# Half blocks of x for the column loop, issued by ScalarE instead of SyncE

## The chip, the cores and the metric

The kernel runs on one core of a Trainium2 chip. A core has five engines that each work through their own list of instructions in order: TensorE (PE, with PEld for its weight loads), VectorE (DVE), ScalarE (ACT), GpSimd (POOL) and SyncE (SP), which only issues transfers and waits. Transfers run on the core's 16 DMA engines. Engines wait for one another, and for transfers, by semaphores. The metric is the time of one execution on the device in microseconds; less is better.

## The reference

For four sequences of 12,608 positions with 128 channels, a long convolution by FFT is multiplied by x, and a mixture-of-experts step then rewrites the 128 positions of each sequence that score highest:

```
h = (relu(pos_emb @ w1) @ w2) * exp(-0.01 * pos)[:, None]
y = irfft(rfft(x * v, 2S) * rfft(h, 2S), 2S)[:, :S]
a = x * y                                    # the "column loop" makes this product
scores = a @ w_gate                          # per sequence
top = argpartition(-scores, 128)[:128]
out = a;  out[top] += sigmoid(scores[top]) * (relu(a[top] @ w1e) @ w2e)
```

## The kernel before

The transform of length 93 * 250 is taken apart into small matrix products. The work of one sequence (b, four of them) falls into two parts.

**Groups.** 32 groups of four channels each, so 128 turns t in all; the loop over t is in the body of the kernel. In one turn each engine does a few operations of different groups:

- PE: the last transform of group i = t - 3 (`f_i`, L546), the middle transform of group t (`dft`, L341), the first transform of group t + 1 (`f_s1`, L481).
- ACT: copies L546's banks out of PSUM (L550, L551), copies half of L341's result (L344, which DVE's L490 needs), copies L481's result to SBUF (two L483, which the next turn's L341 on PE needs). During the turns of sequences 1 to 3 it also carries the search for the 128 highest scores of the sequence before, a round a turn (L871, L874, L887).
- DVE: the product with the filter's spectrum (`f_y`, L497 to L501) and sums and differences (L490, L487).
- POOL: the product x * v (`stage_u`, L324), L508, L509 and two L589.
- SP: per turn two loads of x and v (`load_u`, L318), one or two stores or two loads of the filter's spectrum (L1305, or `load_h`, L330), in three of four turns a move inside SBUF (`put`, L562).

**Column loop.** After the 32 groups, `P1.run` goes over 16 blocks of columns: the closing transform (L636), the product with x (L647), scores (L691, L701), the store (L675). Its x comes by `load_a` (L611) into a ring of buffers. Six of the blocks have buffers that are free early; these are loaded ahead, in 12 half blocks (4 columns each, 112 partitions x 512 values, 224 KB), one each at the end of the turns listed in `LA`: turns 18 to 29 of sequence 0, every second turn from 6 to 28 of sequences 1 to 3. So there are 48 such half blocks. The other blocks are loaded inside `run`.

**What orders the transfers.** Each engine's list is in the order in which the code records it. All transfers that SP issues draw on eight completion semaphores, DMAHW0 to DMAHW7, handed out in turn over the whole program. A transfer takes the next semaphore and waits, before it is issued, until the transfer that used that semaphore last, the eighth one before it, has landed. It also waits for whatever frees its buffer.

Of the kernel before, what the change touches and what calls it, by code (L numbers as in the profile page):

```python
# [30 lines left out]
HB = 4  # L31
# [9 lines left out]
PR, P0, SH = 112, 8, 13  # L41
# [34 lines left out]
AHEAD = [i for i in range(NX + 3) if XB[i] not in XE]  # L76
# [162 lines left out]
def hyena_moe(ctx, tc, xg, x2, pos, bw, ww, wg, mw1, mw2, cs, c1, gx, cf, ci, wm, tk, out):  # L239
    nc = tc.nc  # L240
# [9 lines left out]
    def view(t, off, shape):  # L250
        n = int(np.prod(shape[1:]))
        r = t[:shape[0], off:off + n]
        if len(shape) > 2:
            ax = "abcdefg"[:len(shape) - 1]
            r = r.rearrange(f"p ({' '.join(ax)}) -> p {' '.join(ax)}", **dict(zip(ax[1:], shape[2:])))
        return r
# [57 lines left out]
    def load_u(t):  # L314
        b = t // NG
        if b < B:
            for k, n in enumerate("xv"):
                nc.sync.dma_start(buf(n, t, [NP, XC]), xg[b, :, GC[t], k])  # L318

    def stage_u(t):  # L320
        if t >= B * NG:
            return
        x, v = buf("x", t, [NP, XC]), buf("v", t, [NP, XC])
        nc.gpsimd.tensor_tensor(out=x, in0=x, in1=v, op=ALU.mult)  # L324
# [13 lines left out]
    def dft(t, te, pq):  # L338
        for w in (1, 0):
            for a in range(0, 128, 32):  # L340
                nc.tensor.matmul(pq[w][a:a + 32], lhsT=cf_sb[:, 2 * w + a // NQ, a % NQ:a % NQ + 32],  # L341
                                 rhs=te[:, a // NQ], start=True, stop=True)
        qs = buf("qs", t, [128, HC])
        nc.scalar.copy(out=qs, in_=pq[1])  # L344
        return qs
# [129 lines left out]
    def f_s1(t, dst=None, ps=bank1):  # L475
        u = buf("x", t, [NP, 4, N3])
        te = buf("te", t, [128, 2, 4, N1]) if dst is None else dst
        tps = [view(ps[h], 0, [128, 2, 2, N1]) for h in range(2)]
        for s in range(4):
            for k, c in enumerate(BLK):  # L480
                nc.tensor.matmul(tps[s // 2][c, s % 2], lhsT=u[:, s, c], rhs=c1_sb[:, k], start=True, stop=True)  # L481
        for h in range(2):
            nc.scalar.copy(out=te[:, :, 2 * h:2 * h + 2].rearrange("p e s i -> p s e i"), in_=tps[h])  # L483
        return te.rearrange("p e s i -> p e (s i)")

    def f_u(pq, qs):
        nc.vector.tensor_tensor(out=nat(pq[0]), in0=nat(pq[0]), in1=rev(qs), op=ALU.add)  # L487

    def f_v(pq, qs):
        nc.vector.tensor_tensor(out=nat(pq[1]), in0=rev(pq[0]), in1=nat(qs), op=ALU.subtract)  # L490

    def f_y(t, uv):
        ht = buf("ht", HI[t], [128, 2, HC]) if HS[t] != "hh" else hh[:, GC[t]].rearrange("p e s i -> p e (s i)")
        mt, yz = buf("mt", t, [128, 2, HC]), buf("yz", t, [128, 2, HC])
        for e in (1, 0):
            for o, k in ((mt[:, e], 0), (uv[e], 1)):
                nc.vector.tensor_tensor(out=o, in0=uv[e], in1=ht[:, k], op=ALU.mult)  # L497
        yield yz
        nc.vector.tensor_tensor(out=yz[:, 0], in0=uv[1], in1=mt[:, 0], op=ALU.add)  # L499
        yield yz  # L500
        nc.vector.tensor_tensor(out=yz[:, 1], in0=mt[:, 1], in1=uv[0], op=ALU.subtract)  # L501
        yield yz
# [61 lines left out]
    def turn(i):  # L564

        g, r = i % NG, i % 4
        if i > DIR:
            u = [(t, s) for t in ((i, DIR) if i == DIR + 1 else (i,)) for s in range(4)]
        elif r == 0:
            u = [(i - 1, s) for s in (1, 2, 3)] if g else []  # L570
        else:
            u = {1: [(i, 0), (i, 1), (i, 2)], 2: [(i - 1, 3), (i, 0), (i, 1)], 3: [(i - 1, 2), (i - 1, 3), (i, 0)]}[r]
            if g == NG - 1:
                u += [(i, s) for s in (1, 2, 3)]
        done = []
        for t, s in u:
            f_i(t, s)
            if s == 3:
                done.append(t)
                if t % NG >= NG - 3 and t < DIR:  # L580
                    o, i = parts(t, (0, JM))
                    nc.scalar.copy(out=o, in_=i)
        return done
# [10 lines left out]
    class P1:  # L594
# [7 lines left out]
            self.pw = self.nw = 0  # L602
            self.late = []

        def load_a(self, i, a=0, z=8):
            if i < len(ORD):
                k = ORD[i]
                j0, j1 = blocks[k]
                z = min(z, j1 - j0)
                self.xa[k] = view(arena, XB[i], [128, 8, D])  # L610
                nc.sync.dma_start(self.xa[k][P0:P0 + PR, a:z], x2[self.b, :, j0 + a:j0 + z])  # L611

        def comb(self):
            k = next(self.more, None)
# [622 lines left out]
    te, uv, ys, sd, ph = {}, {}, {}, {}, {}  # L1237
# [7 lines left out]
    def small_steps():  # L1245
        for _ in range(ND):
            bg.hook("d")

    for t in range(NT + LAG):
        g = t % NG  # L1250
        i = t - LAG
        bg.now = t
        done = turn(i) if i >= 0 else []
        if t < NT:
            pq = [bank2[2 - 2 * (t % 2) + e] for e in range(2)]
            spare[0] = [a[:, 512 - NS:] for a in bank1]
            uv[t] = [a[:, :HC] for a in pq]
            qs = dft(t, te.pop(t), uv[t])
            if t == 0:
                rest()  # L1260
            bg.hook("p", 2)
            spare[0] = [pq[0][:, HC:]]
            bg.hook("t", 1)
            spare[0] = [a[:, 512 - NS:] for a in bank1]
            bg.hook("n", 1)
            for k in ((1, 2), (3,), (4,), (5,), ())[t] if t < 5 else (t + 1,):
                if k < NT:
                    te[k] = f_s1(k, ps=banks[6:] if k == 2 else bank1)
            spare[0] = None
            if t != 4:  # L1270
                load_u(t + NU + (t < 4))
            if 0 <= t - 4 < len(fills):
                z = fills[t - 4]
                nc.scalar.activation(out=z, in_=one.to_broadcast([128, z.shape[1]]), func=AF.Copy, scale=0.0)
            o = t - 1 in uv
            if o:
                steps = f_y(t - 1, uv.pop(t - 1))
                y = next(steps)
                next(steps)
            end = t == NT - 1  # L1280
            if end:
                next(steps)
            else:
                small_steps()
            f_v(uv[t], qs)
            if o and not end:
                next(steps)
            if not end:
                bg.hook("e")
            f_u(uv[t], qs)  # L1290
            seam = i >= 0 and i % NG == NG - 1
            now = [k for k in done if seam or end or k % NG == NG - 3]
            done_ = [k for k in done if k not in now]
            for k in now:
                f_c(k)
            if o or t - 1 in ys:
                sd[t - 1] = f_sd(t - 1, y if o else ys.pop(t - 1))
            for k in done_:
                f_c(k, (ALU.subtract,))
            if not seam and t != 4:  # L1300
                stage_u(t + 3 + (t < 4))
            for k in done_:
                f_c(k, (ALU.add,))
            for k in range(4 * (t - 1) // 3, min(4 * t // 3, NG)) if t else ():
                nc.sync.dma_start(hd[:, k], hh[:, k].rearrange("p e s i -> p (e s i)"))  # L1305
            load_h(t + 2)
            for k in due + [k for k in done if k % NG >= NG - 3]:
                put(k, *((JM, NJ) if k % NG >= NG - 3 else ()))
            due = [k for k in done if k % NG < NG - 3]
            for _ in range(0 if end else NE):  # L1310
                bg.hook("e")
            if i >= 0 and i % NG == NG - 1:
                *_, ys[t] = f_y(t, uv.pop(t))
            if t == NT - 1:
                sd[t] = f_last(t, uv.pop(t))
        if t >= NT:
            for k in due:
                put(k)
            due = []
            for k in done:  # L1320
                f_c(k)
        if t == NT:
            bg.drain()
            ex = Experts(picked)
        b = i // NG
        if i >= 0 and i % NG in LA[b]:
            if i % NG == LA[b][0]:
                ph[b] = P1(b)
            k, e = divmod(LA[b].index(i % NG), 2)
            ph[b].load_a(AHEAD[k], e * HB, (e + 1) * HB)  # L1330
        if i % NG == NG - 1 and i >= 0:
            bg.drain("w")
            p1 = ph.pop(b)
            p1.run(ex)
            bg.drain()
            bg = Background(topk_one(b, p1, ex))
# [51 lines left out]
```

## Time and profile before

| | us |
|---|---|
| median of three timed runs | 778.36 (775.6 to 780.43) |
| the profiled execution, its own time | 783.39 |
| its span, first to last instruction | 781.6 |
| PE busy | 760.4 (97% of the span) |
| DVE busy | 684.9 (88%) |
| POOL busy | 619.5 (79%) |
| ACT busy | 572.1 (73%) |

The profiled execution took 5.03 us (0.6%) more than the median, and 1.79 us of it lie outside the span. Busy shares are means over the group turns, the column loops and the two ends of the program. TensorE's granted clock is 0.999 of full speed over the whole run. All transfers of the program stand on one hardware queue that SP feeds, and its packets take 79.8% of the 16 DMA engines' span.

### The profile page before, as it was taken

What the parts mean: (1) busy time and instruction counts of PE and PEld (TensorE: products, weight loads), DVE (VectorE), ACT (ScalarE), POOL (GpSimd) and SP (SyncE); (2) the same over time, 40 slices, a digit from 0 to 9 for tenths busy, and PEclk for the clock granted to TensorE, in tenths of its full rate; (3) what the DMA queues carried; (4) which work ended last, traced back from release to release, by engine and by line L of the source; (5) the groups of instructions that cost most, each with busy time, mean ns of one, the idle gap of its engine ahead of it and who ended that gap; (6) DMA issues with size and microseconds to landing.
All of it is one profiled execution on the core that took longest, in us unless ns stands there. A gap on an engine that the chain in (4) does not pass through costs nothing. (4 is left out here: it accounts for less than half of the span.)

```text
span 781.6 us, 37672 instructions
## 1 busy us (share of the span) xinstructions
PE 760.4 (97%) x15191; PEld 560.6 (72%) x15191; DVE 684.9 (88%) x1549; ACT 572.1 (73%) x2286; POOL 619.5 (79%) x704
## 2 busy tenths in 40 slices
PE   8999999999999999999999999999999999999996
PEld 8999767888853677877834777789536778877356
DVE  7468699989989899989899998989998998997992
ACT  0324567756569989886679898986699888975892
POOL 0200189999989799998888899989997998998873
PEclk9999999999999999999999999999999999999999
DMA  9200269999889979999789999999789899995780
GB/s 323 78 28 3 81 226 297 301 305 288 225 276 286 315 242 290 284 280 270 210 261 304 292 264 279 285 269 265 237 275 330 250 275 270 273 272 163 251 298 26
DMA packets 95649, 190.44 MB, mean 244 GB/s; under 512 B 11952, under 2 KB 70256, under 8 KB 95472
## 3 DMA queue, kind: packets, MB, share of 16 engines
q1 hardware_dynamic: 95216, 187.48, 79.8%
q8 instruction: 121, 1.98, 1.1%
q0 software_dynamic: 256, 0.52, 0.2%
q14 instruction: 56, 0.46, 0.2%
HBM read 135.34 MB, written 41.35 MB: 226 GB/s over the span
## 5 line engine op out<-in xcount | busy, mean ns | idle before, releaser
L546 PE MATMUL b<-ci_sb,arena 128*31 128x126 f32 x6096 | 206.6, 270 | 4.4 <-issue 3.8
L341 PE MATMUL c<-arena,cf_sb 128*32 128x372 f32 x2032 | 201.9, 477 | 3.5 <-issue 2.6
L481 PE MATMUL a<-c_sb,arena 128*32 128x186 f32 x4064 | 202.3, 322 | 2.4 <-issue 2.2
L324 POOL TENSOR_TENSOR arena<-arena 128x500 f32<-128x500 f32 x128 | 162.6, 1271 | 46.1 <-DMA arena<-in_xg_dram 23.9
L546 PEld LDWEIGHTS b<-ci_sb,arena 128*31 128x31 f32 x6096 | 184.0, 109 | 12.9 <-issue 6.9
L508 POOL TENSOR_TENSOR arena<-arena 128x372 f32<-128x372 f32 x127 | 116.5, 917 | 80.6 <-DVE arena L501 72.1
L483 ACT COPY arena<-a 128x372 f32<-128x372 f32 x252 | 119.7, 475 | 80.5 <-PE a L481 75.6
L481 PEld LDWEIGHTS a<-c_sb,arena 128*32 128x32 f32 x4064 | 149.0, 109 | 39.0 <-issue 17.7
L701 ACT ACTIVATE arena<-arena 128x128 f32<-128x128 f32 x490 | 143.8, 295 | 13.0 <-DVE arena L691 12.5
L550 ACT COPY big<-b 128x412 f32<-128x412 f32 x192 | 108.3, 565 | 12.4 <-PE b L546 10.5
L509 POOL TENSOR_TENSOR arena<-arena 128x372 f32<-128x372 f32 x127 | 116.1, 914 | 0.0
L341 PEld LDWEIGHTS c<-arena,cf_sb 128*32 128x32 f32 x2032 | 83.1, 109 | 45.9 <-issue 23.0
L589 POOL TENSOR_TENSOR big<-big,arena 128x184 f32<-128x184 f32 x194 | 112.8, 583 | 1.3
L497 DVE TENSOR_TENSOR c<-c,arena 128x372 f32<-128x372 f32 x188 | 102.4, 545 | 0.0
L497 DVE TENSOR_TENSOR arena<-c,arena 128x372 f32<-128x372 f32 x188 | 100.8, 536 | 0.0
L701 ACT ACTIVATION_READ_ACCUMULATOR arena<-arena 128x1 f32 x490 | 91.7, 187 | 0.0
L490 DVE TENSOR_TENSOR c<-c,arena 128x372 f32<-128x372 f32 x128 | 70.3, 550 | 20.5 <-ACT arena L344 14.2
L621 POOL TENSOR_TENSOR arena<-big 96x512 f32<-96x512 f32 x64 | 79.3, 1267 | 0.1
L636 PE MATMUL a<-big,gx_sb 96*64 96x512 f32 (+2 forms) x448 | 75.9, 474 | 1.4 <-DVE arena L647 0.8
L344 ACT COPY arena<-c 128x372 f32<-128x372 f32 x128 | 60.9, 476 | 14.8 <-PE c L341 14.2
L487 DVE TENSOR_TENSOR c<-c,arena 128x372 f32<-128x372 f32 x128 | 70.0, 547 | 0.2
L499 DVE TENSOR_TENSOR arena<-c,arena 128x372 f32<-128x372 f32 x127 | 68.1, 536 | 0.0
(222 smaller groups left out, 1079.8 us busy)
## 6 DMA issues: line engine op xcount, KB each, us to landing
arena<-in_xg_dram SPq DMA_DIRECT2D x256, 250.0 KB, 5.0
arena<-hd SPq DMA_DIRECT2D x178, 186.0 KB, 5.3
out_dram<-arena SPq DMA_DIRECT2D x60, 448.0 KB, 5.6
arena<-in_x_dram SPq DMA_DIRECT2D x36, 448.0 KB, 5.1
hd<-big SPq DMA_DIRECT2D x32, 372.0 KB, 5.1
arena<-in_x_dram SPq DMA_DIRECT2D x48, 224.0 KB, 5.4
big<-big SPq DMA_DIRECT2D x84, 126.0 KB, 5.0
big<-in_pos_dram SPq DMA_DIRECT2D x7, 496.0 KB, 7.0
```

The lines of the kernel that those rows point to most:

```text
L324: nc.gpsimd.tensor_tensor(out=x, in0=x, in1=v, op=ALU.mult)
L341: nc.tensor.matmul(pq[w][a:a + 32], lhsT=cf_sb[:, 2 * w + a // NQ, a % NQ:a % NQ + 32], rhs=te[:, a // NQ], start=True, stop=True)
L481: nc.tensor.matmul(tps[s // 2][c, s % 2], lhsT=u[:, s, c], rhs=c1_sb[:, k], start=True, stop=True)
L483: nc.scalar.copy(out=te[:, :, 2 * h:2 * h + 2].rearrange("p e s i -> p s e i"), in_=tps[h])
L497: nc.vector.tensor_tensor(out=o, in0=uv[e], in1=ht[:, k], op=ALU.mult)
L508: eng.tensor_tensor(out=nat(sd[:, 0]), in0=nat(yz[:, 0]), in1=rev(yz[:, 1]), op=ALU.add)
L509: eng.tensor_tensor(out=nat(sd[:, 1]), in0=rev(yz[:, 0]), in1=nat(yz[:, 1]), op=ALU.subtract)
L546: nc.tensor.matmul(o3[32 * k:32 * k + NT3, s % 2, e * NJ + js.start:e * NJ + js.stop], lhsT=d[:, e, s, c], rhs=ci_sb[:, e, js], start=True ...
L550: nc.scalar.copy(out=ay[:, GC[t], :NJ + JM, ss], in_=o3[:, :, :NJ + JM].rearrange("p s x -> p x s"))
L589: nc.gpsimd.tensor_tensor(out=d if op == ALU.subtract else a[:, :n], in0=a[:, :n], in1=stg(t)[:, :n], op=op)
L621: nc.gpsimd.tensor_tensor(out=cm[:KP, e].rearrange("p j (g s) -> p j g s", s=4), in0=av[0], in1=av[1], op=op)
L701: nc.scalar.activation(out=x, in_=x, func=AF.Copy, accum_out=self.sc[:, j:j + 1])
```

## The change

`load_a` gets a parameter for the issuing engine, with SyncE as the default, and the call in the group turns passes ScalarE. The calls inside `run` stay on SyncE.

```
-        def load_a(self, i, a=0, z=8):
+        def load_a(self, i, a=0, z=8, eng=nc.sync):
...
-                nc.sync.dma_start(self.xa[k][P0:P0 + PR, a:z], x2[self.b, :, j0 + a:j0 + z])
+                eng.dma_start(self.xa[k][P0:P0 + PR, a:z], x2[self.b, :, j0 + a:j0 + z])
...
             k, e = divmod(LA[b].index(i % NG), 2)
-            ph[b].load_a(AHEAD[k], e * HB, (e + 1) * HB)
+            ph[b].load_a(AHEAD[k], e * HB, (e + 1) * HB, nc.scalar)
```

PE, DVE and POOL keep their lists. ACT's list gains 48 transfers, SP's loses them.

ACT before, between two turns of sequence 1 (L871 and L874 belong to the search's round; `b` is a PSUM bank of L546, `c` of L341, `a` of L481; `ms`, `hi` and `st` hold the search's counts and bounds):

```order
L871 ACTIVATE ms_0_3935,st_3937<-hi_3934,st_3937 128x126 [waits Activation_49]
L874 ACTIVATE st_3937<-tk_sb,st_3937 128x4
L550 COPY big<-b_76 128x206x2 [waits PE_49]
L551 COPY arena<-b_76 128x46x2 [waits Pool_49]
L344 COPY arena<-c_75 128x372 [waits PE_49]
```

ACT of the change, at the same place:

```order
L871 ACTIVATE ms_0_3935,st_3937<-hi_3934,st_3937 128x126 [waits Activation_49]
L874 ACTIVATE st_3937<-tk_sb,st_3937 128x4
L611 DMA arena<-in_x_dram 112x512 [waits DMAHW3_49]
L550 COPY big<-b_76 128x206x2 [waits PE_49]
L551 COPY arena<-b_76 128x46x2 [waits Pool_49]
L344 COPY arena<-c_75 128x372 [waits PE_49]
L483 COPY arena<-a_70 128x2x2x93 [waits PE_49]
L483 COPY arena<-a_71 128x2x2x93 [waits PE_49,Activation_49]
```

The half block's load stands ahead of the next turn's three kinds of copies, with a wait for the last transfer on DMAHW3.

SP before, at the same place of the program:

```order
L330 DMA arena<-hd 128x372 [waits DMAHW1_49,DVE_49]
L330 DMA arena<-hd 128x372 [waits DMAHW2_49,DVE_49]
L562 DMA big<-big 32x1008 [waits DMAHW3_49,Activation_49,Pool_49]
L318 DMA arena<-in_xg_dram 128x500 [waits DMAHW4_49,PE_49]
L318 DMA arena<-in_xg_dram 128x500 [waits DMAHW5_49,Pool_49]
L330 DMA arena<-hd 128x372 [waits DMAHW6_49,DVE_49]
L330 DMA arena<-hd 128x372 [waits DMAHW7_49,DVE_49]
L562 DMA big<-big 32x1008 [waits DMAHW0_49,Activation_49,Pool_49]
L611 DMA arena<-in_x_dram 112x512 [waits DMAHW1_49]
L318 DMA arena<-in_xg_dram 128x500 [waits DMAHW2_49,PE_49]
L318 DMA arena<-in_xg_dram 128x500 [waits DMAHW3_49,Pool_49]
L330 DMA arena<-hd 128x372 [waits DMAHW4_49,DVE_49]
```

SP of the change:

```order
L330 DMA arena<-hd 128x372 [waits DMAHW1_49,DVE_49]
L330 DMA arena<-hd 128x372 [waits DMAHW2_49,DVE_49]
L562 DMA big<-big 32x1008 [waits DMAHW3_49,Activation_49,Pool_49]
L318 DMA arena<-in_xg_dram 128x500 [waits DMAHW4_49,PE_49]
L318 DMA arena<-in_xg_dram 128x500 [waits DMAHW5_49,Pool_49]
L330 DMA arena<-hd 128x372 [waits DMAHW6_49,DVE_49]
L330 DMA arena<-hd 128x372 [waits DMAHW7_49,DMAHW0_49,DVE_49]
L562 DMA big<-big 32x1008 [waits DMAHW0_49,Activation_49,Pool_49]
L318 DMA arena<-in_xg_dram 128x500 [waits DMAHW1_49,PE_49]
L318 DMA arena<-in_xg_dram 128x500 [waits DMAHW2_49,Pool_49]
L330 DMA arena<-hd 128x372 [waits DMAHW4_49,DVE_49]
```

L611 is gone from SP's list, and the semaphores are dealt out a little differently: the following two L318 take DMAHW1 and DMAHW2, and DMAHW3 goes to ACT's load. The last transfer on DMAHW3 before that is the first L562 shown. Before the change the half block took DMAHW1 and waited for the first L330 shown, two transfers earlier.

## Rows read from the trace of the kernel before

**Rows 1.** The page's first part: span, and busy us, share, instructions by engine.
```profile
span 781.6 us, 37672 instructions
PE 760.4 (97%) x15191; PEld 560.6 (72%) x15191; DVE 684.9 (88%) x1549; ACT 572.1 (73%) x2286; POOL 619.5 (79%) x704
```

**Rows 2.** Busy us by engine in four stretches of turns with half blocks.
```profile
core 0: us, PE busy (x) PEld busy (x) DVE busy (x) ACT busy (x) POOL busy (x), PEclk, DMA share, GB/s
170.00:222.00 52.00, 50.72 (x1274) 43.66 (x1270) 47.87 (x104) 32.25 (x81) 48.67 (x60) 1.00 0.91 267
290.00:346.00 56.00, 55.09 (x1392) 44.83 (x1387) 53.34 (x142) 51.33 (x191) 53.90 (x65) 1.00 1.03 284
457.00:529.00 72.00, 70.03 (x1789) 55.50 (x1785) 67.07 (x174) 63.10 (x229) 66.79 (x81) 1.00 0.99 276
623.00:704.00 81.00, 78.15 (x1994) 64.86 (x1990) 74.31 (x191) 68.10 (x239) 75.00 (x90) 1.00 0.97 273
```

**Rows 3.** The page's transfers: the 48 half blocks, KB each, us to landing.
```profile
arena<-in_x_dram SPq DMA_DIRECT2D x48, 224.0 KB, 5.4
```

**Rows 4.** L611 over the run, then within 290 to 346: issue ns min/median/max.
```profile
L611 SPq DMA_DIRECT2D arena<-in_x_dram x88: 322/345/1532, 172.1 to 751.5; - x88
...
L611 SPq DMA_DIRECT2D arena<-in_x_dram x7: 333/420/742, 292.2 to 338.1; - x7
```

**Rows 5.** ACT's timeline, 297.2 to 299.8: start us, us, instruction, idle before.
```profile
297.44 0.28 ACT L874 ACTIVATE st<-tk_sb,st 128x4 f32<-128x4 f32 x1
297.63 0.54 ACT L550 COPY big<-b 128x412 f32<-128x412 f32 x1
...
298.16 0.48 ACT L344 COPY arena<-c 128x372 f32<-128x372 f32 x1
...
299.19 0.47 ACT L483 COPY arena<-a 128x372 f32<-128x372 f32 x1 [0.18 <-PE a L481]
```

**Rows 6.** Timelines of DVE and PE: the operations that need these copies.
```profile
298.91 0.55 DVE L490 TENSOR_TENSOR c<-c,arena 128x372 f32<-128x372 f32 x1
...
300.17 0.50 PE L341 MATMUL c<-arena,cf_sb 128*32 128x372 f32 x4
```

**Rows 7.** SP's timeline, 293 to 300.
```profile
293.63 0.86 SPq L330 DMA_DIRECT2D arena<-hd  x2
294.58 0.51 SPq L562 DMA_DIRECT2D big<-big  x1
...
298.23 0.51 SPq L562 DMA_DIRECT2D big<-big  x1
299.39 0.33 SPq L611 DMA_DIRECT2D arena<-in_x_dram  x1
```

**Rows 8.** Transfers issued around 294.58: KB, us to landing.
```profile
big<-big SPq DMA_DIRECT2D x1, 126.0 KB, 5.9
```

**Rows 9.** L330 in 290 to 346: issues, and DMA to landing.
```profile
L330 SPq DMA_DIRECT2D arena<-hd x30: 326/382/1622, 290.1 to 345.1; - x30
...
DMA to landing us min/median/max: 3.6/5.8/6.6
```

**Rows 10.** The last positive place: ACT's timeline, SP's timeline, L330's landing.
```profile
686.74 0.99 ACT L483 COPY arena<-a 128x372 f32<-128x372 f32 x2
...
683.58 0.86 SPq L330 DMA_DIRECT2D arena<-hd  x2
...
arena<-hd SPq DMA_DIRECT2D x1, 186.0 KB, 5.1
```

**Rows 11.** Waits over the run: us in total, times, longest us.
```profile
ACT arena L483 <- PE a L481: 75.6, 170, 1.3
...
POOL arena L324 <- DMA arena<-in_xg_dram: 23.9, 7, 17.4
```

**Rows 12.** SP's waits in 290 to 346: us in total, times, longest us.
```profile
SPq L330 <- DVE arena L497: 3.3, 8, 0.9
...
SPq L318 <- POOL arena L324: 2.6, 5, 0.7
```

## The prediction

> **What bounds the kernel now.** I read the first part of the page first: PE is busy for 760.4 of 781.6 us, ACT for 73% [rows 1]. The change loads ACT, so the mean would say that there is room. The mean is the wrong reading, so I next cut the span into the stretches in which the 48 half blocks are issued [rows 2]. In 290 to 346 us, the turns of sequence 1 that also carry the search, PE is busy for 55.09 of 56 us (98%), DVE for 53.34 (95%), POOL for 53.90 (96%) and ACT for 51.33 (92%), and the DMA engines are full (share 1.03). The stretches of sequences 2 and 3 look alike, a little looser (ACT 63.10 of 72 and 68.10 of 81). In sequence 0 (170 to 222) there is no search and ACT is busy for 32.25 of 52 us. So PE is the bound, but three other engines and the DMA engines stand within a few per cent of it.
>
> Third, the timelines of one place, the end of ACT's turn at 297.72 us. ACT ends L874 at 297.72 and starts L550 at 297.63, so no time is left between (the two overlap); L344 ends at 298.64 and the second L483 at 299.66 [rows 5]. DVE's L490, which reads L344's result, starts at 298.91, and PE's L341, which reads L483's, at 300.17 [rows 6]. So what comes later on ACT may come 0.27 us later for DVE and 0.51 us for PE, no more.
>
> **What the change removes.** SP loses 48 issues. L611's issue takes 345 ns in the middle and 322 at least [rows 4]; in 290 to 346 the middle one takes 420 with what it waits for. 48 x 0.345 = 17 us of SP's list. Nothing that bounds the kernel waits for SP's loads: POOL waited for x and v 7 times, 23.9 us, of which 17.4 us is one wait, the start of the program [rows 11]. The remaining 6.5 us is the upper bound of what a freer SP gives back. I take nothing of it as a direct gain.
>
> **What it adds on ACT: the issue.** No row shows a transfer issued by ACT. The nearest rows are SP's own issues of the same transfer, 0.32 to 0.35 us without a wait [rows 4]. Lower bound 0: where the engine still works on a copy, the issue may pass beside it. Upper bound: 48 x 0.35 = 17 us, all of it on the path. In ACT's order it stands ahead of L550, L344 and L483, with a slack of 0.27 and 0.51 us behind it [rows 5, 6], so 0.33 us is about what the slack swallows. By itself I cost it at 0, covered by that slack; where a wait comes with it, the slack is used up only once.
>
> **What it adds on ACT: a wait.** This is the term that decides. Every half block waits until the eighth transfer before it has landed, and on ACT everything behind it waits too: L550 and L551 (PE's banks), L344 (DVE's L490), L483 (PE's L341). In the program of the change the place above waits for the last transfer on DMAHW3, the L562 that SP issued at 294.58 us [rows 7]. It landed 5.9 us later [rows 8], at 300.5. ACT is ready at 297.72: a wait of 300.5 - 297.72 = 2.8 us. SP itself came to this half block only at 299.39 [rows 7], 1.7 us after ACT would, and that lag is why the same rule cost SP little. At the last place with a wait ACT ends L483 at 687.73; the L330 that it waits for was issued at 683.58 and landed 5.1 us later, at 688.7: 0.9 us [rows 10].
>
> Read in the same way, 34 of the 48 places have a positive wait, from 0.1 to 3.3 us, 52.7 us together: 2.5 in sequence 0, 20.7, 19.1 and 10.5 in sequences 1 to 3. Some 40 us of it lies in the turns that carry the search, where ACT has the least room [rows 2].
>
> **How much of it reaches the end.** Not all. The waits come every second turn, some 8 us apart. The first makes ACT, DVE and PE late; the transfer that the next one waits for may have been issued before that delay reached SP, so the next wait is shorter by it. Of two neighbours I therefore count the larger: 1.3 + 13.1 + 12.8 + 6.2 = 33.4 us, over 17 pairs. The wait returns after that, because SP doesn't run free: its L330 waits for DVE's L497 and its L318 for POOL's L324 [rows 12], and both follow L490, which follows L344. From this I take off, per pair, 0.42 us for the issue that SP no longer makes ahead of the awaited transfer [rows 4], 0.3 us of slack at the consumers [rows 6] and 0.44 us that ACT idles before L483 anyway (75.6 us in 170 times [rows 11]), and add 0.33 us for the issue: 17 x 0.83 = 14 us. 33.4 - 14 = **19 us**. Bounds: nothing, if the awaited transfers land early; 52.7 us, if each wait is paid in full.
>
> The half blocks themselves are read only after the turns, in the column loop; their 5.4 us to landing [rows 3] stays beside the turns' work, and I cost it at nothing. SP's transfer that comes eight later now waits for ACT's half block. In the example ACT would issue at about 300.5, SP issued its own at 299.39, so that it lands some 1 us later; this stands beside work, as SP lags anyway.
>
> **Sum.** The profiled execution took 783.4 us, 5.0 above the median; 783.4 + 19 = 802 for it, and for the median 778.4 + 19 = **797 us**, 2.4% slower. About 1% (8 us) is what a measurement of this kernel can tell from no change.
>
> **Rivals.**
>
> *The landings give way (not slower).* A later ACT asks for x, v and spectra later, the DMA engines drain, and the transfers land sooner. L330 took 5.8 us to land in the middle, but 3.6 at its quickest [rows 9]. If landings fall by that 2.2 us, a wait of up to 2.2 us is gone; what is left of the larger ones (2.8, 2.5, 3.3, 3.1, 2.6, 3.1 and a few of 2.2 to 2.3) is 0.6 + 0.3 + 1.1 + 0.9 + 0.4 + 0.9 + 0.1 = 4.3 us: 783 us. It decides where the landing falls below about 4 us. For it: the DMA share was only 0.97 in the last stretch, and its waits are half as large. Against it: in 290 to 346 the share is 1.03 [rows 2], the bytes stay the same, and a pace that is slower by 2% empties little.
>
> *Every wait is paid.* If the delay reaches SP before the next awaited transfer is issued, the halving fails: 778.4 + 52.7 less 34 x 0.3 of slack = 821 us. For it: within 290 to 346 SP waits 13 times for DVE or POOL [rows 12], so their delay is soon its own. Against it: the transfer of the example was issued 3.1 us before ACT was ready (294.58 against 297.72), when a delay from the half block before can have reached SP only in part.
>
> *Only the issue moves (no change).* SP saves 17 us, ACT pays 17 us beside PE's work; nothing else changes but 0 to 6.5 us of POOL's waits: 772 to 779 us. The waits read above speak against it. The Trainium skill has it as a rule: "DMA: Bandwidth & Descriptors", section "Issuing engines are not separate DMA queues", says that transfers started by different engines run on the same 16 DMA engines, and that starting them on several engines saves only the sequencer's time for starting them, usually small. By that rule the sum would be about 778 us instead of 797. Its first half fits the full DMA share; its second half leaves out that the issuing engine's list also holds the wait for a completion semaphore, which this case's timelines price at up to 3.3 us a time.
>
> **Chances.** My forecast 0.60 (787 to 812), landings give way 0.19, every wait paid 0.11, only the issue moves 0.10. Range 780 to 818: the upper end takes in most of the third case's lower part, the lower one the first rival; about 0.17 is left out. Faster by over 1% (under 770.6): 0.03, out of the last case. Within 1%: 0.19 + 0.07 less a little that the first rival may exceed, 0.24. Slower by over 1% (over 786.1): 0.73.
>
> **What would show it.** ACT's half blocks should stand in the profile with issues of 1 to 3 us, waits included, in 290 to 350, 457 to 515 and 620 to 680 us, and 0.33 us where there is no wait. DVE's L490 should wait for ACT's L344 by about 20 us more than before, and PE idle by as much; the column loops should not change. The forecast is wrong if PE's idle time stays at 21 us, if the awaited transfers land in under 4 us, or if ACT's issue takes over 0.5 us without a wait.

## The result, and the profile after

The changed kernel took 786.85 us (median of six runs, 785.69 to 789.1) against 779.12 us (775.6 to 781.79) of the kernel before beside it: 1.0104 times as long, 95% interval 1.0073 to 1.0134, **8 us slower**. A second comparison gave 1.0122 (1.0085 to 1.0158). Below, a ratio is turned into us with 777 us, the median of the kernel before in those comparisons.

The first part of the page of the changed kernel, its profiled execution at 785.69 us:

```profile
span 783.9 us, 37679 instructions
PE 762.1 (97%) x15191; PEld 538.9 (69%) x15191; DVE 684.4 (87%) x1549; ACT 570.4 (73%) x2286; POOL 619.8 (79%) x704
```

[rows 1] came from a long execution of the kernel before (783.39 us). A repeat of the unchanged kernel, profiled at 773.77 us, is the better partner:

```profile
span 772.0 us, 37672 instructions
PE 755.8 (98%) x15191; PEld 545.1 (71%) x15191; DVE 683.9 (89%) x1549; ACT 572.8 (74%) x2286; POOL 619.2 (80%) x704
```

Against it PE is idle 5.6 us longer (21.8 against 16.2) and busy 6.3 us longer; in the profile of the second comparison these are 4.5 and 7.7 us. Against [rows 1] the idle time hardly differs (21.2). One profile of each would have shown nothing here.

The four stretches of [rows 2] in the changed kernel, same columns:

```profile
170.00:222.00 52.00, 49.96 (x1250) 40.48 (x1245) 45.45 (x100) 30.32 (x78) 48.45 (x59) 1.00 0.93 278
290.00:346.00 56.00, 54.92 (x1365) 39.09 (x1361) 51.66 (x138) 50.25 (x188) 52.29 (x63) 1.00 0.96 280
457.00:529.00 72.00, 69.94 (x1741) 51.10 (x1736) 66.50 (x172) 61.73 (x225) 66.20 (x81) 1.00 0.93 275
623.00:704.00 81.00, 79.50 (x1998) 56.74 (x1993) 75.46 (x192) 68.65 (x247) 75.35 (x91) 1.00 0.93 273
```

The second of them in the repeat of the kernel before:

```profile
290.00:346.00 56.00, 56.00 (x1440) 43.87 (x1436) 54.06 (x144) 52.84 (x198) 54.72 (x67) 1.00 1.00 288
```

In 290 to 346 the engines get less done: PE 1365 matmuls where it did 1392 [rows 2] and 1440 (repeat), and DVE is busy for 51.66 us instead of 53.34 and 54.06. The DMA share is 0.96 instead of 1.03 and 1.00.

The page's queues and transfers (queue: packets, MB, share; transfer: KB each, us to landing):

```profile
q1 hardware_dynamic: 89072, 176.46, 72.8%
q10 hardware_dynamic: 6144, 11.01, 4.9%
...
arena<-hd SPq DMA_DIRECT2D x178, 186.0 KB, 4.7
...
arena<-in_x_dram ACTq DMA_DIRECT2D x48, 224.0 KB, 4.8
big<-big SPq DMA_DIRECT2D x84, 126.0 KB, 4.7
```

ScalarE's 48 half blocks have a queue of their own (q10) and land in 4.8 us instead of 5.4 [rows 3]; in the repeat of the kernel before it was 5.2. L330 in 290 to 346, where it took 5.8 [rows 9]:

```profile
DMA to landing us min/median/max: 2.9/4.7/5.9
```

This pair of profiles makes the difference look larger than it is: in the same stretch L330 took 5.0 us in the repeat and 5.1 in the second profile of the change. Over the whole run its median is 5.3 and 5.0 us before, 4.7 in both profiles of the change.

The issues of L611 over the run (ns, min/median/max), which answer [rows 4]:

```profile
L611 ACTq DMA_DIRECT2D arena<-in_x_dram x48: 318/318/390, 171.1 to 710.2; - x48
L611 SPq DMA_DIRECT2D arena<-in_x_dram x40: 317/324/1085, 228.3 to 751.1; - x40
```

An issue on ScalarE is 0.32 us. The wait isn't in it: the trace shows it as ScalarE's idle time ahead of the issue. The place of [rows 5] in the changed kernel, on ScalarE, and the transfer that it waits for on SyncE:

```profile
299.45 0.19 ACT L871 ACTIVATION_READ_ACCUMULATOR ms<-hi,st 128x1 bf16 x1
299.54 0.35 ACTq L611 DMA_DIRECT2D arena<-in_x_dram  x1
299.55 0.28 ACT L874 ACTIVATE st<-tk_sb,st 128x4 f32<-128x4 f32 x1
299.93 0.56 ACT L550 COPY big<-b 128x412 f32<-128x412 f32 x1
```

```profile
294.81 0.54 SPq L562 DMA_DIRECT2D big<-big  x1
```

Here 2.8 us were forecast, and there is no wait. ScalarE comes 4.8 us after L562's issue (299.64 - 294.81), not 3.1, and L562 has landed by 299.54, after at most 4.7 us, not 5.9 [rows 8]. A later place, where the wait is there:

```profile
314.89 0.37 ACT L863 ACTIVATE a<-hi,st 128x126 f32<-128x126 int16 x1
316.75 0.32 ACTq L611 DMA_DIRECT2D arena<-in_x_dram  x1
317.11 0.57 ACT L550 COPY big<-b 128x412 f32<-128x412 f32 x1 [1.85 <-DMA big<-big]
```

```profile
311.38 0.51 SPq L562 DMA_DIRECT2D big<-big  x1
```

ScalarE is ready at 315.26, the L562 issued at 311.38 holds it until 316.75, L550 starts 1.85 us late. Read so at all 48 places (start of the issue less the end of ScalarE's instruction before it), 30 waits are over 0.1 us, **26.8 us together** (29.2 in the profile of the second comparison), where 34 and 52.7 were forecast. By sequence they are 9.2, 6.7, 6.5 and 4.4 us (9.8, 7.1, 7.9 and 4.4 in the second profile). Up to the end of the issue ScalarE loses 38.8 us.

The waits that this makes, over the run (us, times, longest), and the same two groups in the repeat of the kernel before:

```profile
ACT arena L483 <- PE a L481: 50.0, 109, 1.3
...
DVE c L490 <- ACT arena L344: 27.6, 39, 3.4
...
ACT big L550 <- DMA arena<-hd: 8.8, 6, 2.1
...
ACT big L550 <- DMA big<-big: 7.6, 5, 3.1
```

```profile
ACT arena L483 <- PE a L481: 67.0, 155, 1.8
...
DVE c L490 <- ACT arena L344: 14.0, 21, 2.1
```

ScalarE now waits for transfers; DVE's L490 waits 13.6 us more for L344; and ScalarE's idle time ahead of L483 shrinks by 17 us (by 25.6 against [rows 11]): that much of the lost time ScalarE would have been idle anyway.

### The profile page after: what moved, and what is told of

The parts are those of the page before. It is cut to its first block, busy times and chain, and to the rows that moved or that the text cites. A ratio compares the mean times of both kernels' runs of the same rounds, so it can differ in the third digit from the quotient of the medians.

```text
span 783.9 us, 37679 instructions
## 1 busy us (share of the span) xinstructions
PE 762.1 (97%) x15191; PEld 538.9 (69%) x15191; DVE 684.4 (87%) x1549; ACT 570.4 (73%) x2286; POOL 619.8 (79%) x704
## 5 line engine op out<-in xcount | busy, mean ns | idle before, releaser
L546 PE MATMUL b<-ci_sb,arena 128*31 128x126 f32 x6096 | 200.0, 270 | 6.1 <-ACT arena L551 2.8
L341 PE MATMUL c<-arena,cf_sb 128*32 128x372 f32 x2032 | 193.4, 477 | 2.3 <-ACT arena L483 1.3
L481 PE MATMUL a<-c_sb,arena 128*32 128x186 f32 x4064 | 193.5, 321 | 0.2
L546 PEld LDWEIGHTS b<-ci_sb,arena 128*31 128x31 f32 x6096 | 177.6, 109 | 17.6 <-issue 5.1
L481 PEld LDWEIGHTS a<-c_sb,arena 128*32 128x32 f32 x4064 | 137.8, 109 | 39.5 <-issue 15.5
L483 ACT COPY arena<-a 128x372 f32<-128x372 f32 x252 | 120.8, 479 | 55.2 <-PE a L481 50.0
L550 ACT COPY big<-b 128x412 f32<-128x412 f32 x192 | 109.1, 570 | 48.7 <-PE c L341 10.2
L341 PEld LDWEIGHTS c<-arena,cf_sb 128*32 128x32 f32 x2032 | 72.5, 109 | 51.0 <-issue 22.8
L490 DVE TENSOR_TENSOR c<-c,arena 128x372 f32<-128x372 f32 x128 | 70.3, 549 | 29.6 <-ACT arena L344 27.6
L501 DVE TENSOR_TENSOR arena<-arena,c 128x372 f32<-128x372 f32 x127 | 67.5, 532 | 0.0
```

The lines of the kernel that those rows point to most:

```text
L546: nc.tensor.matmul(o3[32 * k:32 * k + NT3, s % 2, e * NJ + js.start:e * NJ + js.stop], lhsT=d[:, e, s, c], rhs=ci_sb[:, e, js], start=True ...
L550: nc.scalar.copy(out=ay[:, GC[t], :NJ + JM, ss], in_=o3[:, :, :NJ + JM].rearrange("p s x -> p x s"))
```

## The experiments

Four theories. **A**: the wait in ScalarE's list costs, place by place, what it exceeds ScalarE's room by. **B**: the issue itself fills ScalarE and costs. **C**: SyncE's side costs (other order of transfers, other semaphores, a second queue). **D**: one shift per sequence is paid, whatever the number of waits.

| kernel | ratio to before | 95% | us |
|---|---|---|---|
| kernel before, repeated | 0.9995 | 0.9969 to 1.0021 | -0.4 |
| the change, repeated | 1.0122 | 1.0085 to 1.0158 | +9.5 |
| two activations, SyncE issues | 0.9999 | 0.9973 to 1.0026 | -0.1 |
| a copy that waits for L330, SyncE issues | 1.0063 | 1.0036 to 1.009 | +4.9 |
| the same, waiting a turn's later L330 | 1.1157 | 1.1096 to 1.1219 | +90 |
| ScalarE issues in sequence 0 alone (12) | 1.0020 | 0.9993 to 1.0047 | +1.6 |
| the first 3 of sequences 1 to 3 (9) | 1.0049 | 1.0015 to 1.0084 | +3.8 |
| the last 9 of sequences 1 to 3 (27) | 1.0071 | 1.0039 to 1.0102 | +5.5 |
| the change and two activations | 1.0176 | 1.0127 to 1.0225 | +13.7 |
| ScalarE issues a turn later, before L483 | 1.0232 | 1.0183 to 1.0280 | +18.0 |
| ScalarE issues a turn later, behind L483 | 1.0206 | 1.0158 to 1.0255 | +16.0 |
| SyncE issues a turn later | 1.0001 | 0.9971 to 1.0032 | +0.1 |
| fixed delays, measured lengths | 1.0053 | 1.0019 to 1.0087 | +4.1 |
| fixed delays, forecast lengths | 1.0405 | 1.0367 to 1.0444 | +31.5 |
| measured lengths, a turn later before L483 | 1.0102 | 1.0061 to 1.0144 | +7.9 |
| measured lengths, a turn later behind L483 | 1.0120 | 1.0080 to 1.0161 | +9.3 |

**Both kernels again.**

> The kernel before, unchanged, against itself. All theories: no difference, ratio 1.000 within 0.4%. It gives a second profiled execution of the kernel before: if its turns differ from the first one's by 2 us in all, differences of that size between two profiles say nothing.

> The changed kernel once more, beside the others on the same chip. All theories: 7 to 9 us over the kernel before (1.0%). It gives a second profile of it: if the waits of ScalarE at the 48 issues again sum to 22 to 30 us, they belong to the kernel and not to one execution.

The comparison is sound to some 0.3%, and the change costs 8 to 9.5 us.

**The issue without a wait.** At each of the 48 places, with SyncE issuing:

```
+            for z in range(2):
+                nc.scalar.activation(out=idle[:, z:z + 1], in_=one, func=AF.Identity, bias=one)
```

> SyncE issues the half blocks as before; ScalarE gets two small activations at each of the 48 places (96 of them, about 0.2 us each, so 0.3 to 0.4 us a place), which wait for nothing. Theory A (the wait for the eighth transfer before costs): 0 to 2 us over the kernel before. Theory B (the room that the issue takes on ScalarE, 48 x 0.32 us, costs): 6 to 9 us, as the change. Theory C (SyncE's side costs: other semaphores, a second transfer queue): 0 to 1 us.

Two activations are 0.37 us of ScalarE's list, here at the place of [rows 5]: L550 starts 0.37 us after the first of them, without a wait (lines of kernels with an added definition count one higher, so it is L551 here):

```profile
297.69 0.47 ACT L1333 ACTIVATE idle<-ones 128x1 f32<-128x1 f32 x2
298.06 0.54 ACT L551 COPY big<-b 128x412 f32<-128x412 f32 x1
```

48 x 0.37 = 18 us cost nothing (-0.1 us). B falls.

**The wait without the issue.** SyncE issues; at 33 places ScalarE copies one column of a spectrum that L330 has loaded, and so waits for that landing. The second kernel waits for the L330 of one turn later:

```
+            if b and t + 1 < NT and HS[t + 1] == "hd":      # t + 2 in the second kernel
+                nc.scalar.copy(out=idle[:, :1], in_=buf("ht", HI[t + 1], [128, 2, HC])[:, 1, HC - 1:HC])
```

> SyncE issues the half blocks as before; at the places of sequences 1 to 3 whose next group's spectrum comes by a transfer (33 of 36), ScalarE copies one column out of that spectrum, so that it waits there for the L330 of the turn before, as the changed kernel does at every second place. Theory A: ScalarE waits some 20 us in all there, 5 to 8 us over the kernel before. Theory B: 33 x 0.15 us of room, 0 to 2 us. Theory C: 0 to 1 us.

> SyncE issues all half blocks as before; at the same 33 places ScalarE copies one column of the spectrum that SyncE loads in this very turn, so that it waits for the L330 some 4 us later than in the run with the wait alone (5 us instead of 1 to 2 at the first place). Theory A: each place is paid, 33 x 4 us beyond any room, halved by its neighbour: 60 us and more. Theory D: the first wait of a sequence is 4 us larger, 3 x 4 = 12 us more than the run with the wait alone, 15 to 20 us in all, and the later waits shrink to those of that run.

ScalarE's waits for it, in the first and in the second kernel:

```profile
ACT idle L1333 <- DMA arena<-hd: 28.5, 23, 3.4
```

```profile
ACT idle L1333 <- DMA arena<-hd: 106.0, 32, 5.7
```

Nothing of the transfers' issue is moved, and half of the change's price is there: 28.5 us of waits cost 4.9 us. The price isn't proportional: 106 us cost 90, so 0.86 us a place costs 0.15, and 3.2 us a place costs 2.7. Per place ScalarE's room is about 0.5 to 0.7 us in both (0.7 to 0.9 with the copy's own 0.19 us). D falls here: it expected 15 to 20 us of the second kernel, which cost 90.

But 28.5 us is more than the change waits in these sequences, 17.6 us (19.4 in its second profile), and there the change costs 6.4 to 7.9 us (8 to 9.5 less the 1.6 of sequence 0 below). The intervals overlap. That waits in ScalarE's list cost time is shown; that they are the whole price of the change is not.

**The change in parts.** The last argument of the call:

```
+   nc.scalar if b == 0 else nc.sync                     # sequence 0
+   nc.scalar if b and 2 * k + e < 3 else nc.sync        # first 3 of sequences 1 to 3
+   nc.scalar if b and 2 * k + e >= 3 else nc.sync       # last 9 of sequences 1 to 3
```

> ScalarE issues the 12 half blocks of sequence 0 alone, SyncE the 36 of sequences 1 to 3. In the profiles of the change ScalarE waits 6 to 8 us at these 12, where it carries no search and has room. Theory A (every wait beyond ScalarE's room is paid): 0 to 2 us over the kernel before. If sequence 0 holds what the run with the wait alone left over, 3 to 4 us.

> ScalarE issues the first 3 half blocks of each of sequences 1 to 3 (9 issues), SyncE the other 39. Theory A (paid place by place): 9 of 36 places, so a quarter of the 7 to 8 us of these sequences, 2 us. Theory D (the first waits of a sequence make ScalarE, VectorE and TensorE late against SyncE once, and later waits find them in step): nearly all of it, 5 to 8 us.

> The complement: ScalarE issues the last 9 half blocks of each of sequences 1 to 3 (27 issues), SyncE the first 3 of each and those of sequence 0. Theory A: three quarters, 5 to 6 us. Theory D: again one step per sequence, 5 to 8 us, so that this run and the one with the first 3 together cost clearly more than both at once (13 us against 8).

1.6 + 3.8 + 5.5 = 10.9 us, against 8 to 9.5 for all: the parts add up within their intervals. In sequence 0, without the search, 9.0 us of waits cost 1.6. The first 3 of the other sequences miss both expectations: 3.8 us (1.2 to 6.5) lies between A's 2 and D's 5 to 8. In their trace they have 4.8 us of waits at 7 places, the longest 1.1 us, which the room read above should nearly have swallowed. So A holds for the sum, and not for each part.

**Is it ScalarE's room?** The changed kernel, and the two free activations behind each issue:

> The changed kernel, and at each of the 48 places two small activations on ScalarE behind the half block's issue (0.37 us of ScalarE's list, which by themselves cost nothing when SyncE issued). It tells what swallowed the larger part of the changed kernel's waits. Theory A (ScalarE's own idle time before L550 and L483, 0.5 to 0.8 us a place, pays the first part of each wait): the activations use up that room, so that at the 31 to 34 places with a wait up to 0.37 us more is paid; the time is 8 to 9.5 us for the waits and 5 to 13 more, 13 to 22 us above the kernel before. Rival (the two costs lie at different places or are covered by different work, and simply add): 8 to 9.5 us above it, as the changed kernel.

They cost nothing alone and some 4 to 5.6 us behind the waits, which speaks for waits that had used up the room. The forecast of A (5 to 13 us more) holds at its lower end; the rival's 8 to 9.5 us in all lie just outside the interval (9.9 to 17.5).

**Other places in ScalarE's list.** The call is kept for a turn and made there between L344 and the two L483, or behind them; the third kernel does the latter on SyncE:

```
-            ph[b].load_a(AHEAD[k], e * HB, (e + 1) * HB)
+            late_a.append((ph[b], AHEAD[k], e * HB, (e + 1) * HB))
...
+            for p, *a in late_a:
+                p.load_a(*a, nc.scalar)        # nc.sync in the third kernel
+            late_a.clear()
```

> ScalarE issues the half block one turn later, behind the copies L550, L551 and L344 and ahead of the two L483. By the program it waits for a transfer one or two later in the list than in the changed kernel, and ScalarE comes about 1 us later, so I expect the waits to be of the same size, 20 to 35 us in all. VectorE's L490 now gets L344's result ahead of the wait; only TensorE's L341 stands behind it. If the price was handed on by L344 and L490: under 5 us above the kernel before, and L490's wait for L344 back at some 14 to 18 us. If any place in ScalarE's list hands it on (theory A): 6 to 12 us, with TensorE waiting for L483 in place of it.

> ScalarE issues the half block one turn later, behind the two L483 of that turn, where nothing of that turn stands behind it, only the search's round and the turn after. The awaited transfer is one to three later in the list, ScalarE about 2 us later. Theory A: the wait is of the same size as in the changed kernel and is paid beyond the room of 0.5 to 0.8 us a place: 5 to 12 us above the kernel before. Rival (the place behind L483 is free, as the search's round has slack): 0 to 3 us.

> SyncE issues the half blocks as before, but one turn later, behind the two L318 of that turn: the order of the transfers and the semaphores are near those of the run with ScalarE issuing behind L483, without anything in ScalarE's list. Theory A (only the wait in ScalarE's list costs): 0 to 1.5 us above the kernel before. Theory C (the shifted order of transfers and semaphores costs by itself): 3 us or more.

Of C, the order of SyncE's transfers falls: shifted on SyncE it costs 0.1 us. A second queue without waits on ScalarE was not run. In the trace of the change PE, DVE and POOL wait 45.6 us for transfers, in the repeat of the kernel before 45.3, nearly all of it at one line:

```profile
POOL arena L324 <- DMA arena<-in_xg_dram: 43.0, 5, 21.6
```

```profile
POOL arena L324 <- DMA arena<-in_xg_dram: 45.3, 11, 21.1
```

So no engine but ScalarE waits longer for transfers in the change.

Both other kernels missed: 18 and 16 us, though ScalarE's waits, read as above, are together no longer than in the two profiles of the change (28.8 us at 25 places and 24.4 at 26). PE's waits tell what stands behind. Ahead of L483, then behind it:

```profile
PE c L341 <- ACT arena L483: 10.3, 15, 1.2
```

```profile
PE c L336 <- ACT ms L871: 10.8, 13, 2.4
```

In the first PE's L341 waits directly (1.3 us in the change). In the second the search's round stands behind the wait, and PE's list holds its small matmul L336, which waits for L871; the trace of the change has no such wait. The place only looked free.

**Reading or converting?** With SyncE issuing, small activations of 0.187 us stand at the change's place, as many as fill a given length. `WAITS` holds 48 counts, 205 activations (38.3 us) for the lengths measured in the changed kernel up to the end of the issue, or 367 (68.6 us) for the waits forecast plus 0.33 us an issue. Two more kernels have the measured lengths at the two later places.

```
+            for z in range(WAITS.pop(0)):
+                nc.scalar.activation(out=idle[:, z:z + 1], in_=one, func=AF.Identity, bias=one)
```

> SyncE issues the half blocks as in the kernel before. ScalarE runs small activations in place of the waits: at each of the 48 places as many as fill the time from the end of its last instruction to the end of the issue in the profile of the changed kernel, 205 activations of 0.187 us, 38.3 us in all. If the price of the change is ScalarE's lost time less its room, whatever the wait is for: 6 to 13 us above the kernel before (8 to 9.5 is what the change costs; a room of 0.8 to 1.0 us a place gives 10 to 14). If the price comes from the tie between SyncE's transfers and ScalarE's wait, fixed delays without the tie cost less: 0 to 4 us.

> SyncE issues. The delays on ScalarE have the lengths that the prediction read off the unchanged kernel: the 34 positive waits of 52.7 us, and 0.33 us for the issue at each place, 367 activations, 68.6 us in all. If the forecast failed by reading the waits too long: these delays cost about what was forecast or more, 19 to 37 us. If it failed in converting waits into time: they too cost only 8 to 14 us.

> SyncE issues. The same 205 activations as in the run with delays of the measured lengths, one turn later between L344 and the two L483. ScalarE issuing there cost 16 to 18 us. If the place in ScalarE's list makes the price (TensorE's L341 stands right behind it): 14 to 20 us. If it was the tie to a later landing: as at the change's own place, 6 to 13 us.

> SyncE issues. The same 205 activations one turn later, behind the two L483. ScalarE issuing there cost 16 us. If the place in ScalarE's list makes the price: 13 to 19 us. If it was the tie to a later landing: 6 to 13 us.

Measured lengths cost 4.1 us, forecast ones 31.5. So waits as long as they were read would have cost more than the 19 forecast, not less: the reading failed, and the conversion into time was, at these lengths, too low. A room of 1.0 us a place in sequences 1 to 3 fits both, worked out as the sum of what each delay has above it: 5.5 us of the measured lengths, 30 us of the forecast ones (sequence 0 has more room). The first kernel fell between its two expectations: fixed delays of the change's lengths cost about half of what the change does (the intervals 1.0019 to 1.0087 and 1.0073 to 1.0134 just touch).

At the later places the same delays cost 7.9 and 9.3 us, both in the range expected if the tie (ScalarE waits for a landing, not for a fixed time) makes the price: the place alone doubles it, and with ScalarE issuing there (18 and 16 us) it doubles again. PE's same two groups with fixed delays:

```profile
PE c L342 <- ACT arena L484: 3.1, 6, 0.7
```

```profile
PE c L337 <- ACT ms L872: 6.0, 10, 1.1
```

Why the wait of an issue costs twice a fixed delay is not settled. A late ScalarE makes DVE and POOL late, and through SP's L330 and L318 the next landing; that would do it, but no run here separates it. The kernels also differ in the second queue, and in how the lost time is spread: what exceeds 1.0 us a place in sequences 1 to 3, up to the end of the issue, is 5.6 us in the change (7.3 in its second profile) and 9.3 and 7.0 at the two later places, against 5.5 of the fixed delays. And the kernel in which ScalarE waits for L330 while SyncE issues is tied as well, and cost no more than the fixed delays (4.9 and 4.1 us). TensorE's clock is not the reason: over six runs each, its mean is 0.998 and 0.996 at the later places and 0.999 in the kernel before beside them, up to 2 us of the 16.

## Why the prediction was right in sign and too high by 10 us

**What bounds the kernel.** Right: PE with almost no room, ScalarE's lost time coming out at L490 and L341.

**SP's side.** Right: no gain shows from the 17 us of issues taken off SP, and moving them costs nothing (+0.1 us).

**The issue.** Right at 0: 0.318 us where 0.32 to 0.35 was taken, and 18 us of such work cost nothing. Issues of 1 to 3 us "waits included" do not stand in the profile: the wait is idle time ahead of the issue.

**The wait.** This is the step that failed. The mechanism was right, since the wait moves with the issue; its size was not: 26.8 us at 30 places instead of 52.7 at 34. In sequences 1 to 3 it is 17.6 us instead of 50.3, in sequence 0 9.2 instead of 2.5. It was read off one execution that did not contain it, as a landing that keeps its time less a ScalarE that keeps its time. Neither does. At the 36 places of sequences 1 to 3 the awaited transfer landed on average 5.3 us after its issue in both profiles of the kernel before, and 4.8 and 4.7 in those of the change; ScalarE came 4.2 and 3.9 us after that issue before, and 4.6 and 4.5 in the change. Of the 51 us of waits that the first profile before gives at these places, the new landings alone would leave 33 and the later ScalarE alone 39; both together leave 17. The second queue is not needed for shorter landings: with fixed delays, SyncE issuing everything, L330's median over the run is 4.7 us for the measured lengths and 4.2 for the forecast ones, at DMA shares of 0.94 and 0.82 in 290 to 346. The same reading on the repeat's trace gives some 70 us, so it also varies by a third from one execution of the same kernel to the next.

**How much of it reaches the end.** The 0.83 us taken off a wait fits the runs; counting one wait of two neighbours does not. Taken off each wait by itself, 0.83 us leaves 28 us of the waits as read, where fixed delays of these lengths cost 31.5, and 8.1 us of the waits as they were (10.7 in the second profile), where 8 to 9.5 were measured. So the pairs took away 9 us that would have been paid, and hid about half of the 20 us that the reading had too much. In part the agreement is luck: in the kernels that have them alone, the same rule leaves 4.5 us of sequence 0's waits and 0.5 of those of the first 3, which cost 1.6 and 3.8.

**L490 and PE.** L490's wait rose by 13.6 us against the repeat, not 20. "PE idle stays at 21 us" came true between the two profiles that the prediction had in mind, and would have called the forecast wrong; the repeat shows 5.6 us more idle and 6.3 us more busy time. That test was too weak for a change of 1%.

**The rivals.** "Landings give way" had about half of the cause: the awaited landings fell by 0.5 us to 4.8, not below the 4 at which it decides, and it gave 783 us. "Every wait paid" is refuted for waits of 0.9 us; at 3.2 us a place it comes close (90 of 106 us). "Only the issue moves" is refuted. The Trainium skill's "DMA: Bandwidth & Descriptors" (section "Issuing engines are not separate DMA queues") sees in another issuing engine only sequencer time saved: that time was indeed worth nothing here, but as a forecast of no change the rule fails by 1%.

## What to carry to other kernels

An engine that issues a transfer takes over its waits, and everything behind them in its list: ask for what the issue waits before asking how long it takes. The price of lost time is not proportional to its sum: here 38.3 us in fixed delays of 0.8 us a place on average cost 4.1, and 106 us of waits of 3.2 us a place cost 90. Waits read off a trace that doesn't hold them can be far off in both directions (50.3 us read and 17.6 found, 2.5 read and 9.2 found). To price a place before moving work there, put fixed delays of several lengths in it; here they gave about half of what the moved issue cost.

## What the runs showed of the hardware

ScalarE's issue runs beside its own copy. In the changed kernel:

```profile
206.33 0.47 ACT L483 COPY arena<-a 128x372 f32<-128x372 f32 x1 [0.21 <-PE a L481]
206.36 0.32 ACTq L611 DMA_DIRECT2D arena<-in_x_dram  x1
206.77 0.58 ACT L550 COPY big<-b 128x412 f32<-128x412 f32 x1
```

L611 is issued while L483 runs, and L550 starts as L483 ends: the issue costs the engine no time there.

TensorE's clock can fall behind a stall. With ScalarE issuing behind L483, four stretches of one us (columns as in [rows 2]):

```profile
302.00:303.00 1.00, 0.00 (x0) 0.00 (x0) 1.00 (x3) 0.97 (x5) 1.00 (x3) 1.00 0.42 73
304.00:305.00 1.00, 1.00 (x36) 1.00 (x40) 1.00 (x3) 0.36 (x1) 1.00 (x2) 0.96 1.03 313
305.00:306.00 1.00, 1.00 (x21) 0.92 (x15) 0.10 (x1) 0.46 (x3) 0.81 (x1) 0.50 0.90 266
309.00:310.00 1.00, 1.00 (x42) 0.99 (x35) 1.00 (x4) 0.71 (x2) 0.32 (x1) 1.00 0.70 253
```

PE does no matmul in 302 to 303; the granted clock then goes to 0.50, the lower level of 1.2 GHz, and is back at 1.00 by 309. In the change this is small: its mean clock was 0.998 and 0.996 in the two profiles and 0.9984 over all twelve runs, against 0.9991 over the twelve of the kernel before repeated; 0.0007 of 784 us is 0.5 of its 8 to 9.5 us. In the profile of the kernel with 106 us of waits it was 0.978; 0.022 of its 862.3 us are up to 19 of its 90.
